# A new table of placements, one load moved behind a hold, and a later read of the expert id, in a kernel of attention and mixture of experts on one core

## The chip, the cores and the metric

The kernel runs on 1 core of one Trainium2 chip. The metric is the device time of one execution in microseconds (us). Each timed run carries the TensorE clock that was granted in it (a share of full speed). A run counts as slow when it is over 1.5% above the fastest run of the same kernel; comparisons below use fast runs alone unless they say otherwise.

## The reference

Attention with two softmaxes gives x of shape (8, 576, 512). Then a gate picks one expert for a whole sequence, and that expert's two matrices are applied to all its rows.

```python
q_s = softmax(q, axis=-1); k_s = softmax(k, axis=2)      # q, k, v: (8, 8, 576, 64)
kv  = einsum('bhsd,bhse->bhde', k_s, v)
x   = einsum('bhsd,bhde->bhse', q_s, kv)                 # -> (8, 576, 512)
e_idx = argmax(x.mean(axis=1) @ w_gate, axis=1)          # one expert of 8 per sequence
gate_w = softmax(x.mean(axis=1) @ w_gate)[e_idx]
out[b] = gate_w[b] * (relu(x[b] @ w1[e]) @ w2[e])        # w1: (8, 512, 1024), w2: (8, 1024, 512)
```

With this data the experts of the eight sequences are 2, 3, 3, 1, 3, 3, 4, 6. Sequences 2, 4 and 5 use weights that are already on the chip.

## The kernel before

PE is TensorE (the matmuls), DVE VectorE, ACT ScalarE, POOL GpSimd and SP SyncE, which issues the loads; an eviction takes a finished result out of PSUM, where the matmuls write. Each engine runs its own list of instructions in the order in which the program writes them. The MoE (mixture of experts) of one sequence is a generator that stops at 17 places: 8 in its first layer, 8 in its second and one in the tail. At each stop the program writes the pieces of work for later sequences that a table, `plan`, gives for that place. A place such as 33.38 is read as sequence 33 // 17 = 1, place 16 within it. A half sequence n is 4 of the 8 heads of sequence n // 2.

```python
for b in range(B):
    for m, _ in enumerate(moe(b)):
        run_ticks(NU * b + m + 1)          # NU = 17: writes all pieces of plan up to this place

plan = {
    load: ((0, 4), (3.45, 5), (7.22, 6), ...),               # (place, half sequence)
    mul_q: (..., (54.31, 10), ...),
    gate_step: ((0.05, 1), ..., (53, 4), ...),               # (place, sequence)
    load_w1: (..., (38.09, 3), (59.76, 4), ...),
    hold_loads: ((0.11, 1),),
    fetch: (..., (33.38, 2, w1_all, 0), (33.87, 2, w1_all, 1), ..., (75.68, 4, w2_all, 1), ...),
    ...
}
```

The pieces that the argument touches are these. All loads of q, k and v are issued in order by one queue; `hold_loads(1)` puts a tiny transfer into that queue that reads the last w1 of sequence 1, so that what stands behind it can only leave once those weights have landed.

```python
def hold_loads(b):
    nc.sync.dma_start(out=held, in_=w1_all[64:65, b, ND - 1, F - 8:F])
```

The gate of a sequence is computed by DVE; then POOL reads the expert id, and requests the weights from its own queue. For a sequence whose expert is already in one of the four slots, `fresh` is 0 and the transfers are skipped. In every sequence but the first, DVE then copies the weights in four parts from the slot where they are into the slot of the sequence (for a new expert, the slot onto itself, so that the code is the same):

```python
def gate_step(b):
    ...
    e_val = nc.values_load(eidx[0:1, 0:1], engines=[ET.Pool], ...)     # POOL waits here for the gate
    kw = {}
    if b:
        f_val = nc.values_load(fresh, engines=[ET.Pool], ...)
        kw = dict(cond=(f_val == 1))
    seqs[b].update(zz=zz, nmx=nmx, sidx=sidx, e_val=e_val, kw=kw)

def fetch(b, w_all, part):
    ...
    nc.vector.tensor_copy(out=w_all[:, b % NS, cs, fs], in_=w_all[:, ds(seqs[b]["src"], 1), cs, fs]...)
```

POOL also casts v and multiplies q by the inverse of its sum (`cast_v`, `mul_q`), ACT does exp and the evictions of the MoE from PSUM, DVE the sums, the copies and the gate. The MoE matmuls share three PSUM banks (`mm`), so PE can run at most three evictions ahead of ACT.

## Time and profile before

| | before |
|---|---|
| median of 3 runs before the change | 208.22 us (206.62 to 209.53) |
| profiled execution | 204.87 us, span 203.2 us, granted clock 0.966, fast |
| PE busy | 177.2 us |
| first matmul of the eight MoEs (us) | 30.86, 52.45, 77.47, 100.24, 123.55, 145.99, 165.66, 182.41 |
| last matmul ends | 198.32 us |

The row of starts is the measure that I use throughout: it is read from the timeline of PE, and the difference of two neighbours is the length of one MoE together with the attention work written into it. The slices of the profiled execution show where PE is not full, and where its clock fell. The page cuts the span into 40 slices of 5.08 us; a digit is tenths.

```profile
PE   6877658999899967997977999939999999999990
PEclk9999797999999996999996999999999999999999
```

Counted from 0, the low digits of PE at slices 14 to 15, 20 to 21 and 26 are the stops at about 77, 108 and 137 us, and the 6 of the clock row at 15 and 21 is what follows the first two: the matmuls run slow for a while.

### The profile page before, as it was taken

The page shows a single profiled execution, that of the slowest core. Times are in us where ns is not written, and L with a number is a line of the kernel's source. Part 1 is how long each engine was busy: PE and PEld are TensorE (multiplying, and loading weights), DVE is VectorE, ACT ScalarE, POOL GpSimd, SP SyncE. Part 2 cuts the span into 40 slices and gives each one's busy share as a digit, 9 for nine tenths or more (in the row PEclk, how much of TensorE's full clock was granted, in tenths as well). Part 3 has the DMA queues.
Part 4 walks back from the last instruction along what each step waited for, and adds up shares of the span by engine and source line. Part 5 has one row for each costly group of instructions (what it writes and reads, how often), then busy time and mean ns, then how long its engine had stood idle before and what let it go on. Part 6 is the DMA issues. An engine that isn't in the chain of part 4 may idle for free.

```text
span 203.2 us, 4935 instructions
## 1 busy us (share of the span) xinstructions
PE 177.2 (87%) x1882; PEld 100.4 (49%) x1882; DVE 109.1 (54%) x344; ACT 113.9 (56%) x182; POOL 61.6 (30%) x71
## 2 busy tenths in 40 slices
PE   6877658999899967997977999939999999999990
PEld 6866454554465433554443455525555455445450
DVE  0688865244848836583655475698676542221100
ACT  2667604594689563850951657745566446446540
POOL 2062900740066153456014620470422702300000
PEclk9999797999999996999996999999999999999999
DMA  5999999999999998999997999202892999999055
GB/s 182 375 391 390 354 245 205 148 189 230 382 354 272 334 376 327 292 224 196 258 341 255 387 277 354 101 2 55 217 317 26 159 254 209 164 203 273 10 118 117
DMA packets 29735, 48.58 MB, mean 239 GB/s; under 512 B 4112, under 2 KB 11280, under 8 KB 29712
## 3 DMA queue, kind: packets, MB, share of 16 engines
q1 hardware_dynamic: 19472, 37.76, 55.5%
q0 software_dynamic: 8544, 10.49, 32.0%
q10 hardware_dynamic: 1696, 0.02, 0.6%
q8 instruction: 15, 0.25, 0.5%
q14 instruction: 8, 0.07, 0.1%
HBM read 61.88 MB, written 9.44 MB: 351 GB/s over the span
## 4 chain that ended last, share of the span: by engine, by line
PE 46%; DMA 28%; DVE 11%; issue 5%; ACT 3%; POOL 2%; SPq 1%; POOLq 1%; DVEq 0%; ACTq 0%
PE mm L429 20%; DMA w_all<-in_moe_w_dram 16%; PE mm L447 15%; DMA q_in<-in_q_dram 9%; DVE qs L139 4%; DMA gate<-gt 3%; PE mm L462 2%; PE ht L434 2%; ACT eq L122 2%; PE x L238 2%; PE kv L176 2%; DVE w_all L412 2%; POOL eq L153 1%; PE kv L198 1%; DVE qsi L141 1%
## 5 line engine op out<-in xcount | busy, mean ns | idle before, releaser
L429 PE MATMUL mm<-xt,w_all 128*128 128x512 f16 x256 | 68.1, 397 | 6.6 <-DVE w_all L412 3.1
L447 PE MATMUL mm<-w_all,hsb 128*128 128x512 f16 x256 | 60.1, 379 | 4.8 <-DVE w_all L412 3.4
L438 ACT ACTIVATE hsb<-mm 128x512 f16<-128x512 f32 x64 | 37.5, 596 | 34.1 <-PE mm L429 33.9
L454 ACT ACTIVATE osb<-mm,gate 128x512 f32<-128x512 f32 x32 | 21.7, 686 | 30.8 <-PE mm L447 18.8
L447 PEld LDWEIGHTS <-hsb 128*128 128x128 f16 x256 | 23.0, 98 | 31.0 <-issue 5.0
L153 POOL TENSOR_TENSOR eq<-eq,qsi 128x1152 f16<-128x1152 f16 x13 | 27.5, 2118 | 34.9 <-DVE qsi L141 16.8
L429 PEld LDWEIGHTS <-w_all 128*128 128x128 f16 x256 | 21.3, 101 | 27.0 <-issue 7.6
L412 DVE COPY w_all<-w_all 128x2048 f16 x28 | 23.7, 852 | 18.3 <-DMA w_all<-in_moe_w_dram 15.8
L139 DVE TENSOR_REDUCE qs<-eq 128x18 f32<-128x1152 f16 x16 | 21.5, 1345 | 17.0 <-ACT eq L122 17.0
L130 POOL CAST va<-v_in 128x1152 f16<-128x1152 f32 x15 | 18.0, 1203 | 39.5 <-DMA v_in<-in_v_dram 39.4
L434 PEld LDWEIGHTS <-w_all 128*128 128x128 f16 x256 | 16.7, 100 | 16.2 <-issue 1.9
L122 ACT ACTIVATE eq<-q_in 128x1152 f16<-128x1152 f32 x16 | 18.6, 1160 | 9.8 <-DMA q_in<-in_q_dram 8.5
L249 DVE CUSTOM_DVE_ANT_0 xt<-x,ones_f 128x576 f16<-128x576 f32 x20 | 14.9, 747 | 14.1 <-PE x L239 14.1
L134 ACT ACTIVATE ek<-k_in 128x1152 f16<-128x1152 f32 x16 | 18.6, 1161 | 2.6 <-DMA k_in<-in_k_dram 2.6
L347 POOL DMA_DIRECT2D w_all<-in_moe_w_dram x18 | 8.0, 443 | 37.6 <-DVE nmx L326 14.5
L434 PE MATMUL ht<-xt,w_all 128*128 128x64 f16 x256 | 18.3, 195 | 0.0
L378 PEld LDWEIGHTS <-ident 128*128 128x128 f16 x202 | 13.1, 110 | 2.4 <-POOL ident masks.py:199 1.6
L378 PE MATMUL ht<-blkmask,ident 128*128 128x128 f16 x170 | 12.4, 244 | 1.9 <-POOL blkmask L73 1.9
L238 PE MATMUL x<-qt,kv 128*128 128x512 f16 x32 | 12.8, 401 | 0.7 <-ACT qt L204 0.5
L176 PE MATMUL kv<-va,ek 64*128 64x129 f16 x288 | 11.9, 224 | 0.1
L186 DVE SCALAR_TENSOR_TENSOR kv<-kv,icv,blkmask 128x128 f16<-128x128 f32 x32 | 11.2, 351 | 1.2
L184 DVE RECIPROCAL icv<-kv 128x1 f32<-128x1 f32 x32 | 5.1, 159 | 11.0 <-PE kv L198 10.9
(77 smaller groups left out, 141.4 us busy)
## 6 DMA issues: line engine op xcount, KB each, us to landing
w_all<-in_moe_w_dram POOLq DMA_DIRECT2D x30, 512.0 KB
q_in<-in_q_dram SPq DMA_DIRECT2D x16, 576.0 KB, 6.7
k_in<-in_k_dram SPq DMA_DIRECT2D x16, 576.0 KB, 8.0
v_in<-in_v_dram SPq DMA_DIRECT2D x16, 576.0 KB, 8.5
out_dram<-osb SPq DMA_DIRECT2D x64, 128.0 KB, 5.8
w_all<-in_moe_w_dram POOLq DMA_DIRECT2D x4, 256.0 KB
out_dram<-osb_t SPq DMA_DIRECT2D x16, 64.0 KB, 5.4
gate<-gt ACTq DMA_DIRECT2D x8, 0.5 KB, 5.4
```

Source lines behind the costliest of these rows:

```text
L122: nc.scalar.activation(out=eq.rearrange("p j n d -> p n j d"), in_=ins.pop((n, "q")), func=AF.Exp)
L130: nc.gpsimd.tensor_copy(out=dst, in_=ins.pop((n, "v")))
L134: nc.scalar.activation(out=ek.rearrange("p j n d -> p n j d"), in_=ins.pop((n, "k")), func=AF.Exp)
L139: nc.vector.tensor_reduce(out=qs, in_=halves[n]["eq"], op=ALU.add, axis=AX.X)
L153: eng.tensor_tensor(out=eq, in0=eq, in1=qsi.unsqueeze(3).to_broadcast([128, J, 2, Dh]), op=ALU.mult,)
L378: nc.tensor.matmul(pw, lhsT=ident, rhs=blkmask[:, 0:width], start=True, stop=True)
L412: copy = nc.vector.tensor_copy(out=w_all[:, b % NS, cs, fs], in_=w_all[:, ds(seqs[b]["src"], 1), cs, fs].rearrange("p o c f -> p (o c) f"),)
L429: nc.tensor.matmul(phm, lhsT=w1_sb[:, c, fsl], rhs=xt[:, c, 0:SM], start=(c == 0), stop=(c == ND - 1),)
L434: nc.tensor.matmul(pht[:, fc * ST:(fc + 1) * ST], lhsT=w1_sb[:, c, fsl], rhs=xt[:, c, SM:S], start=(fc == 0 and c == 0), stop=(fc == NF - ...
L438: nc.scalar.activation(out=hsb[:, fc, 0:SM], in_=phm, func=AF.Relu)
L447: nc.tensor.matmul(po, lhsT=hsb[:, fc, st * 128:st * 128 + 128], rhs=w2_sb[:, fc, :], start=(fc == 0), stop=(fc == NF - 1),)
L454: nc.scalar.mul(osb, po, seqs[b]["gate"])
```

## The change

The intent, as the change words it: the table of placements was made anew on a model with random delays, the loads of sequence 2 are held to the w1 of sequence 1, and POOL reads the expert id only when it requests w1. The code part, without the lines of the read that are only moved ("..." marks what is cut):

```diff
 def gate_step(b):
-        sidx = None
+        sidx = fresh = None
...
-        e_val = nc.values_load(eidx[0:1, 0:1], engines=[ET.Pool], ...)
-        kw = {}
-        if b: f_val = ...; kw = dict(cond=(f_val == 1))
-        seqs[b].update(zz=zz, nmx=nmx, sidx=sidx, e_val=e_val, kw=kw)
+        seqs[b].update(zz=zz, nmx=nmx, sidx=sidx, eidx=eidx, fresh=fresh)
 
     def load_w1(b, part=0):
-        kw, slot = seqs[b]["kw"], b % NS
+        eidx, fresh, slot = seqs[b]["eidx"], seqs[b]["fresh"], b % NS
+        if not part:
+            e_val = nc.values_load(eidx[0:1, 0:1], engines=[ET.Pool], ...)
+            kw = {} ... (as above)
+            seqs[b].update(e_val=e_val, kw=kw)
+        kw = seqs[b]["kw"]
```

All places of the table change ("..." marks what is cut):

```diff
-        load: ((0, 4), ...            hold_loads: ((0.11, 1),),
+        load: ((0.27, 4), ...         hold_loads: ((0.05, 1),),
-        sum_q: ... (30.72, 8)         fetch: ... (33.38, 2, w1_all, 0), (33.87, 2, w1_all, 1)
+        sum_q: ... (34.43, 8)         fetch: ... (31.23, 2, w1_all, 0), (31.78, 2, w1_all, 1)
-        fetch: ... (75.68, 4, w2_all, 1)
+        fetch: ... (67.36, 4, w2_all, 1)
-        mul_q: ... (54.31, 10)        gate_step: ... (53, 4)     load_w1: ... (59.76, 4)
+        mul_q: ... (56.18, 10)        gate_step: ... (52.5, 4)   load_w1: ... (56.46, 4)
-        load_w1: ... (38.09, 3), (90.93, 6)     gate_spread: ... (42.91, 2)
+        load_w1: ... (45.44, 3), (84.37, 6)     gate_spread: ... (40.44, 2)
-        fetch: ... (98.39, 6, w1_all, 0), (102.33, 6, w1_all, 1), (104.12, 6, w2_all, 0)
+        fetch: ... (93.63, 6, w1_all, 0), (104.28, 6, w2_all, 0), (105.87, 6, w1_all, 1)
```

## The prediction

> **What bounds the kernel now.** I read the page first (busy shares, slices, DMA row), then the timeline of PE from end to end, then the chain that ended last, and last the timelines of POOL, DVE and the DMA queue around each stop of PE. Busy shares and slices, from the page:
>
> ```profile
> PE 177.2 (87%) x1882; PEld 100.4 (49%) x1882; DVE 109.1 (54%) x344; ACT 113.9 (56%) x182; POOL 61.6 (30%) x71
> DMA  5999999999999998999997999202892999999055
> ```
>
> PE is the busiest engine, and the DMA engines are nearly as full: nine tenths in almost every slice, with a hole around slices 25 to 29 (about 124 to 146 us). So PE sets the end, and it stops where data comes late. A whole MoE of one sequence without interruption takes from 182.48 to 198.3, 15.8 us; eight are 126.6 us. The attention pieces that PE does after the first MoE matmul at 30.86 add about 20 us (12 half sequences of 1.38, gates, the rest of sequence 1). 30.9 + 126.6 + 20 is 178, but PE ends at 198.3: some 20 us are stops and slow matmuls. These are the stops (the timeline of PE; in brackets the idle time and what ended it):
>
> ```profile
> 30.86 1.02 PE L429 MATMUL mm<-xt,w_all 128*128 128x512 f16 x4 [2.59 <-DMA w_all<-in_moe_w_dram]
> 54.49 1.02 PE L429 MATMUL mm<-xt,w_all 128*128 128x512 f16 x4 [0.90 <-ACT osb L454]
> 77.47 1.89 PE L429 MATMUL mm<-xt,w_all 128*128 128x512 f16 x4 [3.12 <-DVE w_all L412]
> 96.78 1.02 PE L447 MATMUL mm<-w_all,hsb 128*128 128x512 f16 x4 [1.36 <-ACT osb L454]
> 107.97 0.66 PE L198 MATMUL kv<-ident,eq 64*128 64x64 f16 x18 [2.37 <-POOL eq L153]
> 137.13 1.02 PE L447 MATMUL mm<-w_all,hsb 128*128 128x512 f16 x4 [3.07 <-DVE w_all L412]
> ```
>
> After the stops at 77 and 108 the matmuls also run slow for a while (four in 1.89 us where 1.03 is usual). The chain of waits shows how the early ones hang together:
>
> ```profile
> 20.16 10.57 DMA w_all<-in_moe_w_dram
> ...
> 36.15 8.86 DMA w_all<-in_moe_w_dram
> 45.02 0.78 SPq L382
> 45.90 6.72 DMA q_in<-in_q_dram
> ```
>
> The first w1 takes 10.57 us to land, the second 8.86; the queue of loads is held behind the second (line 382), and then q of the third sequence takes 6.72 us. Two stops have a cause that is no transfer, which the timelines of POOL and DVE show:
>
> ```profile
> 93.77 1.16 POOL L130 CAST va<-v_in 128x1152 f16<-128x1152 f32 x1
> 105.79 2.12 POOL L153 TENSOR_TENSOR eq<-eq,qsi 128x1152 f16<-128x1152 f16 x1 [10.87 <-PE kv L176]
> ```
>
> ```profile
> 133.01 4.07 DVE L412 COPY w_all<-w_all 128x2048 f16 x2 [0.34 <-DVE qsi L141]
> ```
>
> POOL does nothing from 94.9 to 105.8. In its instruction order the read of the expert id of sequence 4 stands before this multiplication, and the gate of sequence 4 is only done on DVE at 105.4: POOL waits for a number that it doesn't need until the weights are requested. PE then waits 2.37 us for the product. At 133 DVE copies weights that the next matmuls need, at the last moment, and beside POOL's multiplication.
>
> **What the Trainium skill says.** "Trainium Architecture — The Big Picture", Inside one NeuronCore: every engine has its own instruction stream and synchronizes only through semaphores; so within a stream a wait holds all that follows. The POOL lines agree (10.87 us). "DMA: Bandwidth & Descriptors", Queues, rings and completion order: each DMA engine goes round-robin between the queues that have work. Agrees: w1 of sequence 0 needed 10.57 us beside queued loads, that of sequence 7, requested at 171.58 with no loads left, is copied at 179.79, 8.2 us. "TensorE: Matmul & The Clock Gate", What's actually happening: idle for a window of about 3.4 us that runs freely, the array falls to half its clock. The trace agrees on the size (1.89 for 1.03) and on the chance in it: idle 3.12 at 77 was followed by slow matmuls, 3.07 at 137 was not. "GPSIMD Engine Reference", Specifications: its SBUF interfaces are shared with VectorE. The copies of L412 take 0.69 us mostly, and up to 2.5 us at 133 beside POOL.
>
> **The change part by part.** No arithmetic is added or removed; the order program shows the same number of rows on PE, POOL and SP. What moves:
>
> (a) Loads of half sequence 4 (q, k, v, 1.77 MB) now stand behind the hold. Before, they were queued from 11.75 to 16.5. Loads moved 37.76 MB in 55.5% of 203 us with the stores, which is 335 GB/s, so 1.77 MB cost 5.3 us of all DMA engines, just when w1 of sequence 0 was on its way. PE had finished its other work at 28.27 and waited to 30.86. Without this load w1 should land at about 26 to 28: estimate **-2.5 us**. Everything behind, the gate of sequence 1 and its w1, moves by as much: w1 of sequence 1 at about 42.5.
>
> (b) The price: q of half 4 now leaves at about 43.4 and, with the 6.72 us seen, lands at 50.1. Before, exp of half 4 ran at 40.5 without a wait. On ACT the new place of that exp is ahead of the last output scaling of sequence 0, so PE runs out of its three PSUM buffers and waits till about 51.9. The replaced stop was at 54.49, so (a) is kept here, but more waits follow: v of half 4 lands at about 53.3 (before, v of half 5 at 55.8 for a load sent at 45.9), cast 1.2 and multiplication 2.1 end at 56.6, where PE wants it at 54.9; and a wait for exp of half 5 and half 9. Estimate **+4 us** in all, with one slow start of the clock.
>
> (c) The copies of weights for sequence 2 now precede the sum of half 8 on DVE. The stop at 77 (3.12 us and 1.5 slow) is made of that sum's wait for q. Estimate **-4.5 us**.
>
> (d) POOL reads the id at the request. The multiplication of half 10 stands ahead of the request for sequence 4: the stop at 108 (2.37 and some 1.7 slow) goes: **-4 us**.
>
> (e) Copies for sequence 5 are placed some four steps earlier: the stop at 137 goes: **-3 us**. The gate values are sent earlier relative to use: the stop at 96.8 goes: **-1.4 us**.
>
> (f) w1 of sequence 3, whose expert is new in these data, is now asked for 5.5 places before its use instead of 12, after the multiplication of half 9, and the loads of halves 10 to 13 are placed closer to it. POOL isn't tied to PE's place; I trace it to about 87.5 (it was 86.45), while PE would want it at about 95. With round-robin against loads I give it 12 us: PE waits for it at moe 3, **+4 to +6 us** with the clock.
>
> (g) w1 and w2 of sequences 6 and 7 are asked for earlier (6.6 and 4.7 places for 6, three for 7). Before, they just made it (0.35 us of wait at 174.4). If the middle gets faster, this keeps them from being the next stop: about 0.
>
> Sum: -2.5 -0.9 (replaced) +4 -4.5 -4 -3 -1.4 +5 = -7.3. I follow PE forward as a check: moe 1 goes on at 51.9, moe 2 starts at 75, moe 3 at 100.8, and then without stops 15.8 per sequence plus 1.38 per half and gates: moe 7 ends near 190, and with the 4.9 us of tail 195; with 2 to 3 us of slow clock 197.5. The span was 203.2, so -5.7 to -7.3. The timed median 208.2 is 3.3 above the profiled execution (204.87); I don't know where those 3.3 were lost, and carry them over: 208.2 - 6.2 = **202.0 us**.
>
> **The rivals.** First: DMA is the bound, and the order of placements only shifts who waits. For it: nine tenths in nearly all slices up to 120 us; moving 1.77 MB behind the hold makes the supply of the middle later. Against: the hole from 124 to 146 us, which earlier requests can fill. Then the gain at (a) is eaten at (b) and (f): 206 to 209. Second: w1 of sequence 3 becomes the one large stop, with DVE blocked behind the copy that waits for it (that copy stands right after the request in DVE's order): 10 us instead of 5, 207 to 211. Third: the plan is robust as meant, the timed runs of before lose their extra 3.3 us to chance delays, and after doesn't: 195 to 198.
>
> **Range and chances.** The line for faster by over 2% is 204.1. My middle lies 2 us below it; the sum has four gains that I trust (a, c, d, e) and two losses that I size badly (b, f), each by 3 us or so. Range 195.5 to 208.5. Faster 0.63, within 2% 0.31, slower 0.06.
>
> **What will show it.** Right: the first MoE matmul at about 28.3; w1 of sequence 1 landing near 42.5; no POOL gap ahead of the multiplication of half 10; no DVE copy ending a PE stop in moe 4; a stop at the start of moe 3 ended by w1 or its copy; continuous PE from there to the end. Wrong: the first MoE matmul still at 30 or later, which takes away (a); stops in moe 1 of over 5 us; the stop at moe 3 over 7 us; or w2 of 6 or w1 of 7 ending a stop.

## The result, and the profile after

A ratio here and below is the mean time of one kernel's fast runs over the mean of the other's fast runs of the same rounds, so it is not quite the ratio of the medians that stand beside it.

| | before | after |
|---|---|---|
| median (range), 4 runs each | 207.42 us (206.33 to 209.53) | 200.56 us (197.69 to 205.25) |
| ratio of fast runs | | 0.958 (0.948 to 0.968): faster |
| profiled execution | 204.87 us, fast | 201.92 us, slow |

Of the four runs of after, 197.69 and 199.2 were fast, and 201.92 and 205.25 slow. The profile of after thus shows a slow execution. I ran the unchanged new kernel again (called a_again below), and its profile fell on a fast run of 198.81 us. After's own page, in the rows that answer to those of before:

```profile
PE 176.9 (88%) x1882; PEld 100.8 (50%) x1882; DVE 113.0 (56%) x344; ACT 113.5 (57%) x182; POOL 63.6 (32%) x71
...
PE   6978496999989998998399999999999968999990
PEclk9988999999999999999879999999999996999997
DMA  5999799999999799799999996976379999973055
```

The work is the same (1882 matmuls, 177 us). The stops of before at those slices are gone, and the hole in the DMA row at slices 24 to 29 is partly filled (697637 tenths for 920289). In their place stand a stop at slice 19 (98 us) and one at slices 32 to 33 (165 us). The fast profile of the same kernel has them as well, shorter. This is its timeline of PE (start, duration, engine, line, operation, and in brackets the idle time and what ended it; lines of the new kernel have numbers higher by 3):

```profile
52.37 1.02 PE L432 MATMUL mm<-xt,w_all 128*128 128x512 f16 x4 [1.60 <-ACT osb L457]
57.01 0.44 PE L198 MATMUL kv<-ident,eq 64*128 64x64 f16 x18 [0.91 <-POOL eq L153]
...
81.60 0.35 PE L293 MATMUL x<-wg_sb,pooled 128*1 128x8 f32 x8 [1.15 <-ACT xt L247]
...
97.97 0.38 PE L238 MATMUL x<-qt,kv 128*128 128x512 f16 x1 [1.25 <-DVE pooled L249]
109.45 1.89 PE L450 MATMUL mm<-w_all,hsb 128*128 128x512 f16 x8 [0.99 <-DVE w_all L415]
164.21 1.04 PE L432 MATMUL mm<-xt,w_all 128*128 128x512 f16 x4 [1.48 <-DVE gt L395]
```

And the slow profile, the timeline of PE of after at the same two late stops:

```profile
98.20 0.38 PE L238 MATMUL x<-qt,kv 128*128 128x512 f16 x1 [3.64 <-DVE gt L395]
98.44 1.68 PE L432 MATMUL mm<-xt,w_all 128*128 128x512 f16 x4
...
165.76 1.04 PE L432 MATMUL mm<-xt,w_all 128*128 128x512 f16 x4 [2.27 <-DVE gt L395]
...
166.75 1.72 PE L432 MATMUL mm<-xt,w_all 128*128 128x512 f16 x4
```

In this pair the two late stops are longer in the slow execution, and each is followed by slow matmuls (1.68 and 1.72 us for four, where 1.03 is usual). That is no rule for slow executions: at 52 us the slow profile waits only 0.30 us where the fast one waits 1.60, and the slow profile of a_copy6 below has a stop of 3.38 us with matmuls at full speed behind it (1.02). The releaser named in brackets is the last one that the profile saw; at 98 and at 165 the instructions named stand on DVE right behind copies that had waited for weights, and the chain that ended last in after names those weights:

```profile
86.02 10.67 DMA w_all<-in_moe_w_dram
...
150.58 13.73 DMA w_all<-in_moe_w_dram
```

The starts of the eight MoEs tell where the time went. The last row is the fast profile of the new kernel, 6.3 us ahead at the end:

| start of MoE (us) | 0 | 1 | 2 | 3 | 4 | 5 | 6 | 7 | last matmul ends |
|---|---|---|---|---|---|---|---|---|---|
| before | 30.86 | 52.45 | 77.47 | 100.24 | 123.55 | 145.99 | 165.66 | 182.41 | 198.32 |
| after (slow profile) | 29.23 | 49.98 | 73.85 | 98.44 | 118.72 | 139.91 | 159.39 | 179.36 | 195.27 |
| after, run again (fast) | 28.86 | 49.61 | 74.21 | 98.21 | 117.97 | 139.16 | 158.63 | 176.13 | 192.05 |
| lead of the last over before | 2.0 | 2.8 | 3.3 | 2.0 | 5.6 | 6.8 | 7.0 | 6.3 | 6.3 |

About 2 us of lead are there before the first MoE, it stays at 2 to 3 until MoE 3 starts, MoE 3 and MoE 4 add 4.8 (2.0 to 6.8), and then nothing more comes. So the trace alone suggests that the hold at the start and the faults of order in MoE 3 and 4 make the gain. The experiments test this.

### The profile page after: what moved, and what is told of

Read it like the earlier page. It is cut to its first block, busy times and chain, and to the rows that moved or that the text cites. A ratio compares the mean times of both kernels' runs of the same rounds, so it can differ in the third digit from the quotient of the medians.

```text
span 200.1 us, 4935 instructions
## 1 busy us (share of the span) xinstructions
PE 176.9 (88%) x1882; PEld 100.8 (50%) x1882; DVE 113.0 (56%) x344; ACT 113.5 (57%) x182; POOL 63.6 (32%) x71
## 4 chain that ended last, share of the span: by engine, by line
PE 39%; DMA 25%; DVE 21%; issue 5%; ACT 3%; SPq 2%; POOL 1%; POOLq 0%; DVEq 0%; ACTq 0%
PE mm L432 13%; PE mm L450 13%; DMA w_all<-in_moe_w_dram 12%; DMA v_in<-in_v_dram 5%; DMA k_in<-in_k_dram 5%; DVE qs L139 4%; PE ht L381 4%; DMA q_in<-in_q_dram 3%; DVE w_all L415 3%; PE kv L176 2%; DVE score L311 2%; DVE xt L249 2%; PE x L238 2%; SPq L117 2%; PE ht L437 2%
## 5 line engine op out<-in xcount | busy, mean ns | idle before, releaser
L432 PE MATMUL mm<-xt,w_all 128*128 128x512 f16 x256 | 67.3, 394 | 2.6 <-DVE gt L395 2.3
L153 POOL TENSOR_TENSOR eq<-eq,qsi 128x1152 f16<-128x1152 f16 x13 | 28.5, 2194 | 33.4 <-DVE qsi L141 31.5
L415 DVE COPY w_all<-w_all 128x2048 f16 x28 | 22.6, 816 | 26.8 <-DMA w_all<-in_moe_w_dram 23.3
L130 POOL CAST va<-v_in 128x1152 f16<-128x1152 f32 x15 | 18.9, 1261 | 35.7 <-DMA v_in<-in_v_dram 35.6
L176 PE MATMUL kv<-va,ek 64*128 64x129 f16 x288 | 12.4, 229 | 0.3 <-DVE gt L395 0.3
L176 PEld LDWEIGHTS <-ek 64*128 64x128 f16 x288 | 9.4, 100 | 3.8 <-issue 2.4
```

Source lines behind the costliest of these rows:

```text
L130: nc.gpsimd.tensor_copy(out=dst, in_=ins.pop((n, "v")))
L153: eng.tensor_tensor(out=eq, in0=eq, in1=qsi.unsqueeze(3).to_broadcast([128, J, 2, Dh]), op=ALU.mult,)
L176: nc.tensor.matmul(kps[g][:, 0:129], lhsT=ek[r, j], rhs=va[r, j], start=(j == 0), stop=(j == J - 1),)
L415: copy = nc.vector.tensor_copy(out=w_all[:, b % NS, cs, fs], in_=w_all[:, ds(seqs[b]["src"], 1), cs, fs].rearrange("p o c f -> p (o c) f"),)
L432: nc.tensor.matmul(phm, lhsT=w1_sb[:, c, fsl], rhs=xt[:, c, 0:SM], start=(c == 0), stop=(c == ND - 1),)
```

## The experiments

My theory: a few faults of order carry the gain (the early read of the expert id on POOL, and copies that stand too late on DVE), and the load behind the hold, the late w1 of sequence 3 and the copy of sequence 6 are small or cost something. The rival: the transfers are the bound, so order only shifts who waits, and a single fault that is mended gives its gain back at the next wait. A third reading was that the load behind the hold (2 us of lead at once) is the source. Names beginning with b_ are edits of before, with a_ of after. The runs came in three calls (the third, with b_copy2, b_copy4, b_fixes_gate and a_all, on another chip); each call compares with its own runs of before, whose medians were 207.74, 205.29 and 205.82 us. Ratios of different calls are compared below with that reserve.

### The unchanged new kernel again (a_again)

No edit. The texts of what was expected stand here, as in all sections below.

> The changed kernel, unaltered, once more, since its profiled run was of the slow state. Theory (the gain comes from removed stops of PE, four of them): a fast profile shows the first MoE matmul at about 29, no stop at the start of moe 2, in moe 3 before the transposes of half 10, or in moe 4, and two stops: at the start of moe 3 (w1 of sequence 3, about 3.6 us) and in moe 6 (about 2.3 us). Time 198 to 201 us, 0.95 to 0.965 of before. Rival (the two slow first matmuls after a stop are chance, and half of the gain is chance of the clock): the ratio falls to 0.97 or above.

Measured: 198.49 us (195.98 to 203.01), ratio 0.962 (0.952 to 0.972). Its interval agrees with that of the result. Its clock column also says something about the spread: the five runs from 195.98 to 199.27 had 0.989 to 0.996, and the slowest (203.01) had 0.968. Of before, the fastest run of this call (203.8) had 0.975 and the slowest (209.38) 0.934. A spread like the 3.3 us that stood unexplained in the prediction thus goes together with a lower granted clock, but not always (a_w3_alone has a run of 200.57 at 0.989 beside one of 195.56 at 0.988); which is cause and which is effect, these runs don't tell.

### Before, with the late read of the expert id alone (b_read_late)

```diff
 # before.py, table unchanged
-    gate_step: e_val, f_val = values_load(...)
+    load_w1, part 0: e_val, f_val = values_load(...)
```

> The kernel before with one part of the change alone: GpSimd reads the expert id at the w1 request, not at the gate. Theory: in the table of before the multiplication of half 10 no longer waits for the gate of sequence 4; the stop at 108 (2.37 us and 1.7 us of slow matmuls) goes, so the time falls by 3 to 4 us, ratio 0.98 to 0.985. Rival (the supply of inputs bounds the middle, the stop only moves to moe 4): ratio over 0.993.

Measured: 203.98 us (201.77 to 205.62), ratio 0.986 (0.977 to 0.996), so 1.4% or 2.9 us. The timeline of PE has no stop at 108 any more, MoE 3 takes 19.2 us instead of 23.3, and MoE 4 24.1 instead of 22.4. The remaining stop there is the one of the copy:

```profile
134.66 1.59 PE L450 MATMUL mm<-w_all,hsb 128*128 128x512 f16 x4 [3.12 <-DVE w_all L415]
```

So 4.1 us were won in MoE 3, and 1.7 were given back in MoE 4, where after the same idle time as before (3.12 us, before 3.07) the matmuls now ran slow.

### After, with the early read put back (a_read_early)

```diff
 # after.py, table unchanged
-    load_w1, part 0: e_val, f_val = values_load(...)
+    gate_step: e_val, f_val = values_load(...)
```

> The changed kernel with that part undone: GpSimd reads the expert id at the gate. In the new table the multiplication of half 10 comes behind the gate of sequence 4 and ahead of its w1 request, so GpSimd waits for that gate (104.5 in the trace) and ends the product at about 107.5, while PE wants it at 109.0; the product of half 13 is delayed to about 132 where PE wants it at 131.4. Theory: the new table has slack there, so the time rises by 0 to 1.5 us. Rival (the late read is what the whole gain rests on): it rises by 4 us or more.

Measured: 202.02 us (198.74 to 203.46), ratio 0.975 (0.964 to 0.986) where the unedited kernel has 0.962. That is 1.3%, 2.6 us, more than I expected, though the two intervals overlap. The timeline of POOL in the two kernels shows the wait come back; first with the late read (a_again), then with the early one (a_read_early):

```profile
101.59 2.11 POOL L153 TENSOR_TENSOR eq<-eq,qsi 128x1152 f16<-128x1152 f16 x1 [6.63 <-PE mm L432]
```

```profile
106.15 2.31 POOL L153 TENSOR_TENSOR eq<-eq,qsi 128x1152 f16<-128x1152 f16 x1 [14.04 <-ACT hsb L438]
```

The multiplication of half 10 is 4.6 us later. But PE doesn't stop for it in this profile: the product ends at 108.46, and PE takes it at 110.97. What PE loses here stands at the start of MoE 3, where it waits behind the copy of w1 of sequence 3 (1.25 us in a_again):

```profile
99.47 0.58 PE L238 MATMUL x<-qt,kv 128*128 128x512 f16 x1 [4.84 <-DVE pooled L249]
```

The request for this w1 leaves POOL at 86.24 (85.63 in a_again, 85.35 in after). The profile fell on a slow run, and after's slow profile has 3.64 us at the same stop, so the way in which the early read costs the 2.6 us is not shown.

### Before, with the copies for sequence 2 moved ahead (b_copy2)

```diff
-    fetch: (33.38, 2, w1_all, 0), (33.87, 2, w1_all, 1)
+    fetch: (30.1, 2, w1_all, 0), (30.2, 2, w1_all, 1)      # ahead of sum_q (30.72, 8)
```

> The kernel before with one order mended: on VectorE the two copies of w1 for sequence 2 stand ahead of the sum of half 8. Theory: the stop at the start of moe 2 (3.12 us and about 1.5 us of slow matmuls) goes, the other stops stay; ratio 0.978 to 0.986 (3 to 4.6 us). Rival (moe 2 then waits for the product of half 8 or 9, which lands when it did): under 1.5 us, ratio over 0.993.

Measured: 204.34 us (203.28 to 207.68), ratio 0.997 (0.990 to 1.004): 0.6 us, not distinguishable from nothing. Yet the stop at 77 is gone; MoE 1 takes 21.0 us instead of 25.0. The timeline of PE shows what took its place:

```profile
83.82 0.44 PE L198 MATMUL kv<-ident,eq 64*128 64x64 f16 x18 [1.29 <-POOL eq L153]
94.66 1.02 PE L447 MATMUL mm<-w_all,hsb 128*128 128x512 f16 x4 [1.83 <-ACT osb L454]
105.89 0.43 PE L198 MATMUL kv<-ident,eq 64*128 64x64 f16 x18 [2.42 <-POOL eq L153]
```

PE arrives 3.2 us sooner at MoE 2 (74.29 for 77.47), and there it waits for the product of half 8 (1.29, through POOL) and longer for a gate value that is still in transit (1.83, before 1.36); the third line is the stop of before at 108, which this edit leaves. The first is, by the trace, again a matter of order. The multiplication of half 8 has its inputs at 75.8, but in this table it stands on POOL behind the cast of half 9, which waits for v:

```profile
80.53 1.17 POOL L130 CAST va<-v_in 128x1152 f16<-128x1152 f32 x1 [3.97 <-DMA v_in<-in_v_dram]
81.65 2.12 POOL L153 TENSOR_TENSOR eq<-eq,qsi 128x1152 f16<-128x1152 f16 x1
```

In the new table this multiplication stands ahead of that cast (34.56 and 41.2). At MoE 3 PE is 2.1 ahead, and it keeps 2.0 to the end of this profile (196.28 for 198.32). So a part of the wait moved, as the rival has it; how much of the rest is gain, the interval (-2.0 to +0.8 us) leaves open.

### Before, with the copy of the second half of w2 of sequence 4 moved ahead (b_copy4)

```diff
-    fetch: (75.68, 4, w2_all, 1)
+    fetch: (69.5, 4, w2_all, 1)
```

> The kernel before with one order mended: on VectorE the second copy of w2 for sequence 4 stands ahead of the sums of halves 12 and 13. My prediction took the copy at 133 for one of sequence 5; by the order it is the one of sequence 4. Theory: the stop in moe 4 (3.07 us) goes, ratio 0.985. Rival (the weights of sequences 6 and 7, asked for at the same time as before, take its place near the end): ratio over 0.995, with a stop of 2 us or more in moe 6.

Measured: 204.29 us (201.49 to 205.06), ratio 0.989 (0.981 to 0.997): 1.1%, 2.3 us. The stop at 137 of 3.07 us has become one of 1.47, and MoE 4 takes 20.8 us for 22.4 (in a profile of a slow run). This also settles which copy PE waited for: two stand together at 133 in DVE's order, first one of sequence 5 and then the one of sequence 4 that PE needs. The one of sequence 5 stays where it was, takes 2.50 us, and the work behind it on DVE ends what is left of the stop; DVE first, then PE:

```profile
134.42 2.50 DVE L412 COPY w_all<-w_all 128x2048 f16 x1 [0.34 <-DVE qsi L141]
```

```profile
137.80 0.38 PE L238 MATMUL x<-qt,kv 128*128 128x512 f16 x1 [1.47 <-DVE qt L206]
```

### Before, with these three together (b_fixes)

Edit: the three edits above, applied to before. Nothing else of the new table.

> The kernel before with three orders mended and nothing of the load order changed: the late read; the copies of w1 for sequence 2 ahead of the sum of half 8 on VectorE; the second copy of w2 for sequence 4 ahead of the sum of half 12. Theory (the three stops at 77, 108 and 137 were faults of order within an engine and independent of each other): the gain of the late read (2.9 us) plus 3.1 to 4.6 plus about 3 adds up, 9 to 10 us, ratio 0.952 to 0.957, as good as the whole new table. Rival (the stops stand in for a lack of input: with one away, the next stop or the next landing takes its place): 4 to 6 us, ratio 0.97 to 0.98.

Measured: 198.99 us (197.42 to 201.53), ratio 0.967 (0.956 to 0.977): faster. That is 6.9 us by the call's median of before; the single edits sum to 2.9 + 0.6 + 2.3 = 5.8. So the gains add up, as far as these intervals can tell, and the three make most of what the whole table makes (0.958 and 0.962 in its two measurements, so 7.9 to 8.7 us of 207). The rival claim that each mended fault is given back at the next wait falls for the two in MoE 3 and 4: these take 19.2 and 20.9 us here, for 23.3 and 22.4 in before. What is left in the middle of b_fixes is a wait for the gate value, which the timeline of ACT shows (7.05 us of idle ACT, and PE stopped for 2.61):

```profile
94.89 0.69 ACT L457 ACTIVATE osb<-mm,gate 128x512 f32<-128x512 f32 x1 [7.05 <-DMA gate<-gt]
```

### The same, with the gate value of sequence 2 sent earlier (b_fixes_gate)

```diff
 # b_fixes
-    gate_spread: (42.91, 2)
+    gate_spread: (36.0, 2)
```

> The kernel with the three orders mended, and the gate value of sequence 2 sent to all partitions seven places earlier. Theory: the stop of 2.61 us in moe 2, where ScalarE waits for that value, goes, and the time falls by 2 to 2.6 us against the three mended orders, to about 196.5. Rival (moe 3 waits for w1 of sequence 3 instead): under 1 us.

Measured: 200.16 us (198.34 to 204.37), ratio 0.974 (0.967 to 0.980). The wait is gone, and no gain in time shows beside b_fixes (0.967). Its profile fell on a slow run, in which other stops stand in MoE 2 and MoE 4:

```profile
84.80 0.34 PE L293 MATMUL x<-wg_sb,pooled 128*1 128x8 f32 x8 [1.61 <-ACT xt L247]
...
134.94 0.58 PE L238 MATMUL x<-qt,kv 128*128 128x512 f16 x1 [3.05 <-DVE qt L206]
```

The second stands behind the same copy of sequence 5 as in b_copy4 (2.50 us on DVE, at 131.56). MoE 2 itself takes 22.1 us here and 25.8 in b_fixes, so it is shorter; MoE 1 and MoE 4, which the edit doesn't touch, are 2.9 and 3.6 us longer. Why no time is won is therefore not shown.

### Before, with the load of half sequence 4 behind the hold (b_load4_held)

```diff
-    load: ((0, 4), ...
+    load: ((0.12, 4), ...       # hold_loads stands at 0.11
```

> The kernel before with the load of half 4 moved behind the hold, and nothing else of the table. Theory: the first MoE matmul comes at about 28.5 instead of 31, but ScalarE, whose exp of half 4 stands after the sixth block of moe 0, stops there till q lands at about 50; PE runs out of PSUM buffers at about 38 and waits some 11 us, so the time rises by 6 to 9 us, ratio 1.03 to 1.045. Rival (the load order alone carries the gain): it falls by 2 us or more.

Measured: 213.47 us (212.32 to 214.29), ratio 1.040 (1.024 to 1.057): 8 us longer. The first MoE starts at 28.16 instead of 30.86, a gain of 2.7 us, and then ACT, which has the exp of half 4 ahead of the evictions of MoE 0, stands still for 12.05 us until q lands. PE fills its PSUM banks and stops; ACT first, then PE:

```profile
50.87 1.16 ACT L122 ACTIVATE eq<-q_in 128x1152 f16<-128x1152 f32 x1 [12.05 <-DMA q_in<-in_q_dram]
```

```profile
53.12 1.10 PE L447 MATMUL mm<-w_all,hsb 128*128 128x512 f16 x2 [10.83 <-ACT hsb L438]
```

So the hold is no gain in itself. In the new table exp, sum and multiplication of half 4 were moved back with it (exp_q from 5.5 to 14.79), and ACT waits there for q 1.59 and 2.89 us in the two profiles.

### After, with the load of half 4 ahead of the hold (a_load4_first)

```diff
-    load: ((0.27, 4), ...
+    load: ((0.045, 4), ...      # hold_loads stands at 0.05
```

> The changed kernel with the load of half 4 put back ahead of the hold; nothing else. Theory: w1 of sequence 0 lands later and the first MoE matmul goes back from 29.0 to about 31, while the wait for q of half 4 on ScalarE (1.6 us of PE at 52) and the one for the product of half 4 (0.9) go; the two sides nearly cancel, so the time is within 1.5 us of the changed kernel. Rival (holding the load is where much of the gain is): it rises by 2.5 us or more.

Measured: 199.14 us (196.16 to 201.74), ratio 0.961 (0.931 to 0.991). The interval is wide, but the trace is plain. The first MoE starts at 31.93 instead of 28.86 (+3.1 us), and MoE 1 takes 21.8 us instead of 24.6 (-2.8): the stops at 52 and 57 are gone.

```profile
31.93 1.02 PE L432 MATMUL mm<-xt,w_all 128*128 128x512 f16 x4 [3.22 <-DMA w_all<-in_moe_w_dram]
```

All fourteen profiles agree on this wait: in the six with half 4 behind the hold PE never waits for w1 at the first MoE, in the eight without it always (1.72 to 4.59 us). The start itself moves less surely, from 30.86 to 31.94 without and 27.69 to 31.63 with it; the latest of these, a_copy6, is late because its transposes ahead of the MoE run at a lower clock (0.73 from 20 to 28 us). The hold moves one wait of some 3 us from the start to MoE 1.

### After, with the copies for sequence 6 in the order of use (a_copy6)

```diff
-    fetch: (104.28, 6, w2_all, 0), (105.87, 6, w1_all, 1)
+    fetch: (104.2, 6, w1_all, 1), (104.28, 6, w2_all, 0)
```

> The changed kernel with one copy moved on VectorE: the second half of w1 of sequence 6 is copied ahead of the first half of w2, not behind it. Theory: the stop in moe 6 (2.27 us, and about 1.6 us of slow matmuls behind it) comes only from VectorE's order, as w1 had landed some 11 us before; it goes, and the time falls by 2.3 to 3.9 us against the changed kernel (about 197). Rival (w1 itself was late, or the end is set by w2 of sequence 6, which landed at 164.4): PE stops later instead, at the start of the second layer of moe 6, and the gain is under 1 us.

Measured: 198.19 us (195.42 to 200.22), ratio 0.956 (0.947 to 0.966) beside 0.962 of the unedited kernel: 1.2 us by the ratio, which the intervals don't resolve. The cause of the stop at 165 is shown, though. In a_again the timeline of DVE reads:

```profile
152.41 0.69 DVE L415 COPY w_all<-w_all 128x2048 f16 x1 [0.39 <-DMA w_all<-in_moe_w_dram]
162.85 1.29 DVE L415 COPY w_all<-w_all 128x2048 f16 x2 [4.48 <-DMA w_all<-in_moe_w_dram]
```

and in a_copy6:

```profile
154.06 0.69 DVE L415 COPY w_all<-w_all 128x2048 f16 x1 [0.51 <-DMA w_all<-in_moe_w_dram]
159.84 0.67 DVE L415 COPY w_all<-w_all 128x2048 f16 x1
164.90 0.69 DVE L415 COPY w_all<-w_all 128x2048 f16 x1 [4.39 <-DMA w_all<-in_moe_w_dram]
```

The first copy waits for the transfers of w1 and runs at 152 and 154; by the program these transfers bring the whole of w1, so its second half can be copied from then on. In a_again its copy stands behind a copy of w2, which lands at 162.85, and PE stops for 1.48 us. In a_copy6 it runs at 159.84, and MoE 6 takes 15.8 us without a stop, where it took 17.5 and, in the slow profile of after, 20.0.

### The same, with w1 of sequence 3 asked for earlier (a_w3_alone)

```diff
 # a_copy6
-    load_w1: (45.44, 3)   load_w2: (46.84, 3)   load: (38.12, 10)   cast_v: (46.37, 10)
+    load_w1: (41.9, 3)    load_w2: (41.95, 3)   load: (44.0, 10)    cast_v: (57.0, 10)
-    exp_q: (47.44, 10)  exp_k: (48.9, 10)  sum_q: (51.26, 10)  fetch: (45.8, 3, w1_all, 0)
+    exp_q: (53.5, 10)   exp_k: (55.2, 10)  sum_q: (54.5, 10)   fetch: (47.3, 3, w1_all, 0)
-    kvt_step: (58.72, 10)  x_step: (61.85, 10, 0)
+    kvt_step: (60.3, 10)   x_step: (62.2, 10, 0)
```

> The changed kernel with the copy of sequence 6 in order, and w1 and w2 of sequence 3 asked for ahead of the product of half 9, the load of half 10 sent only after the first store of moe 2, and the uses of half 10 placed later. Theory (w1 of sequence 3 is late because it shares the DMA engines with the loads of halves 10 and 11): w1 is asked for at about 84 and is there in 9 us instead of 10.7, the stop at the start of moe 3 (3.4 to 3.6 us in two profiles, 1.25 in a third) goes, and the time falls by 2 to 4 us against the changed kernel, to about 195. Rival (the DMA engines are full there whatever the order): half 10 is late instead, PE waits in moe 3 for its product, and the time is the same within 1 us.

Measured: 197.69 us (195.56 to 200.57), ratio 0.963 (0.953 to 0.972). The request leaves POOL at 82.75 instead of 85.63 us (a_again), and the start of MoE 3 has no stop, where a_copy6 has one of 3.38 us (in its slow profile) and a_again one of 1.25. But there are now small stops behind it; the timeline of PE:

```profile
104.38 1.02 PE L450 MATMUL mm<-w_all,hsb 128*128 128x512 f16 x4 [0.70 <-DVE w_all L415]
...
117.45 1.02 PE L432 MATMUL mm<-xt,w_all 128*128 128x512 f16 x4 [1.24 <-ACT osb L457]
```

Its single profile has the shortest span of all profiles (193.9 us), but the ratio doesn't differ from that of a_copy6. That the late w1 makes the stop is shown; which of the two edits brings it in time, the earlier request or the load of half 10 out of its way, is not separated, and that mending it is worth time is not shown.

### All of these on the new kernel (a_all)

Edit: a_w3_alone and a_load4_first together.

> The best of what was seen: the changed kernel with the copy of sequence 6 in order, w1 and w2 of sequence 3 asked for earlier and alone, and the load of half 4 ahead of the hold. Theory (holding half 4 costs in moe 1 and 2 what it gains at the start, so the two variants are equal): 196 to 198 us, within 1 us of the variant with the load held (197.7). Rival (the parts add): 195 or less.

Measured: 196.75 us (195.44 to 199.16), ratio 0.959 (0.953 to 0.965). It has the lowest median of all kernels, but the new kernel itself has ratios of 0.958 and 0.962. I don't claim that it is faster. In its profile, as in that of a_load4_first, the first MoE waits for w1 (1.76 us at 31.94), and MoE 6 runs without a stop.

## Why the prediction was right or wrong

The prediction was right: it said 202.0 us in a range of 195.5 to 208.5, with a change of -6.2 us, and the time came out at 200.56 us, 6.9 below the median of before taken with it. But the sum was right with terms that were partly wrong, and so partly by luck. In its own order:

| step | predicted | shown |
|---|---|---|
| (a) first MoE earlier | -2.5 | -1.6 and -2.0 in two profiles; no wait for w1 in any with the hold |
| (b) price in MoE 1 | +4 | two stops of 1.60 and 0.91; +2.8 for MoE 1 by a_load4_first |
| (c) copies for sequence 2 | -4.5 | -0.6 alone (interval -2.0 to +0.8) |
| (d) late read on POOL | -4 | -2.9 alone; undone in the new table 2.6 longer |
| (e) copy in MoE 4 | -3 | -2.3 alone |
| (e) gate value | -1.4 | no gain seen in b_fixes_gate |
| (f) w1 of sequence 3 | +4 to +6 | a stop of 1.25 (fast profile) or 3.64 and slow matmuls (slow profile) |
| (g) weights of sequences 6 and 7 | 0 | a stop of 1.48 or 2.27 and slow matmuls |

**(a) and (b)** had the right mechanism: w1 of sequence 1 was in at 43.28 us (the hold's own transfer starts then; 42.5 was predicted), and q of half 4 landed at 49.64 (50.1 predicted; ACT starts its exp then). The two nearly cancel in the trace, and a_load4_first shows why: it is one wait that is moved. As far as its wide interval tells, the part is no source of the gain, and without the moves around it it costs 8 us.

**(c)** is the term that failed most. I took a stop of 3.12 us with its slow matmuls and counted all of it as gain. The stop did go. But MoE 2 behind it met other waits (the product of half 8, which stood behind the cast that waits for v of half 9, and the gate value), so of 3.2 us at the start of MoE 2 about 2 were left from the start of MoE 3 to the end of the profile, and 0.6 in the time. The gate value in (e) brought no gain that could be seen either. In this stretch the prediction's first rival is right in part: some of the wait moved, though one of the new waits is a fault of order too and not a bound of the transfers.

**(d) and (e)** hold, each a little smaller than predicted. What the prediction said of POOL literally, no gap ahead of the multiplication of half 10, is not what came: POOL still idles 6.63 us there. But now it waits for its own inputs and is done before PE needs the product. What (e) named wrongly is the sequence: the copy that PE needed belonged to sequence 4 and moved from 75.68 to 67.36, while the one of sequence 5 ahead of it in the pair was placed later, at 77.09 instead of 75.66.

**(f)** was the right mechanism, sized too high. In after the transfer left at 86.02 us (87.5 predicted) and took 10.67 us to land (12 predicted). A small slip stands in its text: the old request was 12.9 places ahead of its use, not 12. The times that the prediction gives for the weights of sequences 0 and 7 (10.57 and 8.2 us) fit a sharing of the DMA engines between queues, but they don't show in which order the queues are served.

**(g)** predicted nothing, and missed that the new table puts the copy of the second half of w1 behind a copy of w2. I had compared when the weights were asked for, not the order of the copies that wait for them. In the fast profile this costs 1.5 us. One of the prediction's own signs of being wrong came true here: the landing of w2 of sequence 6 ends a stop, through that copy. Its sign of being right, a continuous PE from the start of MoE 3 to the end, did not come (0.99 us at 109 and 1.48 at 164).

The sum came out because the misses have both signs: (c) and the gate value together were 5.3 too hopeful (5.9 predicted, 0.6 shown), (b) was 1.2 too dark and (f) some 3 to 5 in the fast profile. This is not a full account: with the -2.0 and the two stops of a_again for (a) and (b), and the fast profile for (f) and (g), the right column adds up to about -2.6 us, or -3.5 with the -0.9 for the replaced stop that the prediction also counts, where 6.9 were measured. The parts taken one by one leave some 3 us without a place.

What is shown beyond this sum: three faults of order, mended in before, are together worth 6.9 us (b_fixes), most of what the whole new table is worth. What stays open: whether the rest comes from the table's other moves at all, since 0.967 and 0.962 are within each other's intervals; what the two copies are worth inside the new table, where only the read was put back; and why the granted clock differs between runs of one kernel.

## What to carry to other kernels

Where engines run fixed streams, look first for a wait that stands in a stream ahead of work that doesn't need it (a register read, a copy), and move the wait to the place that uses its result; two such moves were worth 2.3 and 2.9 us here. Before counting a stop as gain, ask what the engine meets next: the stop of 3.12 us at 77 was worth 0.6 when it alone was mended. The hold that lets one transfer go first moved a wait here rather than removing it, and cost 8 us while the users of what was held stayed in their places.

## What the Trainium skill lacked or had wrong

- "TensorE: Matmul & The Clock Gate", What's actually happening: it puts the fall to half the clock after at least one idle window of about 3.4 us. In these traces stops of 2.37 us (before, at 108) and 2.27 us (after, at 165.76) were followed by slow matmuls (1.89 and 1.72 us for four, where 1.03 is usual), in the second case after one block at full speed (1.04), while one of 3.07 us (before, at 137) was followed by none. In a_copy6 even one of 3.38 us (at 100.47) was followed by none. The length of one stop alone doesn't tell which.
- "SBUF — State Buffer", SBUF: two separate sides: it says that GpSimd and a DVE instruction in a two-port mode or with two SBUF inputs take a shared port pair as an exclusive lock for a whole instruction. The traces fit this, and show a case that is easily overlooked, an instruction of eight elements in the path from the gate to the request of the weights. It takes 0.22 us in all its seven executions in before; in after four of the seven take longer, 0.77 to 1.81 us, and the longest ends with POOL's product. DVE and POOL of after (start and duration):

```profile
126.59 1.81 DVE L311 TENSOR_SCALAR score<-hist,efl 1x8 f32<-1x8 f32 x1
```

```profile
126.27 2.12 POOL L153 TENSOR_TENSOR eq<-eq,qsi 128x1152 f16<-128x1152 f16 x1 [0.24 <-DVE mx L299]
```

- No page gives the price of a transfer that a condition skips. In a_again POOL's four skipped requests for the weights of sequence 4 stand at 105.01, 105.48, 105.92 and 106.38 us, so about 0.45 us of POOL's stream each, though each is shown busy for 0.04 us only.
